# Layer norm's input of units 1 and 2: from TensorE's transposes to VectorE's 32 by 32 turns through DRAM, with a new order table

## The chip, the cores and the metric

The program runs on one core of a Trainium2 chip. The metric is the device time of one execution in microseconds (us). Engines: TensorE (PE), VectorE (DVE), ScalarE (ACT), GpSimd (POOL) and SyncE (SP, which here issues all DMAs).

## The reference

Attention with pooled keys and values (8 batches, 8 heads, 576 positions, 64 wide), then two blocks on the 4608 x 512 rows that it gives. Cut to what matters here:

```python
k_p = k.reshape(B, H, S // 8, 8, D).mean(axis=3)       # v_p likewise
attn = softmax(q @ k_p.T / sqrt(D))
x = (attn @ v_p) as 4608 rows of 512
h = x @ w_in                                           # 512 -> 1024
e = h * softmax(h)
ln = (e - mean(e)) / sqrt(var(e) + 1e-6) * g_ln
x = ln @ w_out                                         # 1024 -> 512
out = ((x @ w1) * (x @ w2)) @ w3 @ w_out2
```

## The kernel before, in words

Every product of float32 numbers is made of three products of rounded halves (high by high, high by low, low by high), so each operand of PE has a high and a low tile (winh, winl, xh, xl, lnh, lnl, gwh, gwl).

The first stage, up to about 590 us, works in 18 **units** of 256 rows, each of two halves (row blocks) of 128 rows. Attention runs two groups ahead in the same stage: per group it turns the queries (`pq`, L598), makes scores (`sc`, L617), their maximum and exponentials (L635, L638), divides (on DVE, L653 and L654, and POOL, L658 and L665), transposes the result on PE (`pt`, L683 and L686), splits it (ACT L690 and L691, DVE L694 and L695), and multiplies by the values (`av`, L722), whose result is split (L216, L217) and copied (L729) as xh and xl. Beside it DVE, ACT and POOL convert weights, those of the last block (w1, w2) in 16 "kept" pieces (L289 to L304), which go to DRAM.

For one half of a unit, `Rows` does this: `chunk` multiplies x by w_in in four steps (L753, tile h, one pair of banks for all halves); `exp` takes the maximum (DVE, L761) and the exponential (ACT, L762); `solu` multiplies (DVE, L768, tile e) and sums squares (ACT, L771). The second product needs e with its 1024 columns on the partitions, and there are two ways:
- **On PE**, `Unit.transpose` (L833): four 128 x 128 transposes into one PSUM bank, an ACT copy that rounds (L836, tile lnh) and a DVE subtraction (L837, tile lnl). A unit takes four such groups.
- **Turned**, for units in TURNED: `turn` lets DVE turn 32 x 32 blocks of e (L777) into a tile that also receives the squares of `solu` and exists once; `send` writes it to DRAM (L784, on SP); three slots later `fetch` reads it back in four DMAs that put the blocks in their places (L791); `part` then rounds it on ACT (L823) and subtracts on DVE (L824).

`Unit.chunk` makes the second product (L847 to L849, 48 matmuls of 256 columns for half of the output columns), `store` copies it out (L859) and sends it (L860).

The program is written by **slots**, 16 to a unit, in the pattern of HEAVY: four slots for the first half's chunks of the unit, four for one half of the second product (x), four for the second half's chunks, four for the other half of the second product (y). For a unit below AT_ONCE both halves of its second product stand in the next unit's slots; for a later one the first half stands in the next unit's last four slots, and the second in the unit after. So with AT_ONCE = 3 the x slots of unit 4 hold no second product.

The order in which each engine gets its instructions is then set by hand: `issue_order` reads ISSUE_ORDER, one list for each engine. An entry "skip:count" moves on by skip in the order of the slots and takes the next count instructions. Each engine, and SP's queue of DMAs, works its list in order, so an instruction that waits holds up all behind it.

Of the kernel before, what the change touches and what calls it, by code (L numbers as in the profile page):

```python
# [128 lines left out]
def attention_moe_kernel(  # L129
# [106 lines left out]

    SLOTS = 16
    LEAD = 2  # L240
    HEAVY = "hhhhxxxxHHHHyyyy"
    AT_ONCE = 3
    TURNED = range(AT_ONCE, NU - 1)
    events = {}
    now = None

    def put(slot, fn, *args, first=5):
        assert now is None or slot > now
# [1299 lines left out]
```

## Time and profile before

| | us |
|---|---|
| median of 3 runs | 1176.77 (1175.39 to 1178.05) |
| the profiled execution, its own time | 1180.64 |
| its span, first to last instruction | 1178.8 |
| PE busy in the span | 1138.8 |
| DVE, ACT, POOL busy | 918.6, 545.3, 526.0 |

Busy time of an engine is time in which it executes; times of a row count from the span's start. In a window the number behind x is that of instructions, and the granted clock is a share of TensorE's full speed. "<-" behind idle time names what ended it.

### The profile page before, as it was taken

What the parts mean: (1) busy time and instruction counts of PE and PEld (TensorE: products, weight loads), DVE (VectorE), ACT (ScalarE), POOL (GpSimd) and SP (SyncE); (2) the same over time, 40 slices, a digit from 0 to 9 for tenths busy, and PEclk for the clock granted to TensorE, in tenths of its full rate; (3) what the DMA queues carried; (4) which work ended last, traced back from release to release, by engine and by line L of the source; (5) the groups of instructions that cost most, each with busy time, mean ns of one, the idle gap of its engine ahead of it and who ended that gap; (6) DMA issues with size and microseconds to landing.
All of it is one profiled execution on the core that took longest, in us unless ns stands there. A gap on an engine that the chain in (4) does not pass through costs nothing. (4 is left out here: it accounts for less than half of the span.)

```text
span 1178.8 us, 20225 instructions
## 1 busy us (share of the span) xinstructions
PE 1138.8 (97%) x7210; PEld 1023.1 (87%) x7210; DVE 918.6 (78%) x1376; ACT 545.3 (46%) x1399; POOL 526.0 (45%) x482
## 2 busy tenths in 40 slices
PE   6898989999999999999989999999999989999998
PEld 4688878999989899999989888888888878999998
DVE  5899879889777775696669769989785677988972
ACT  5665657576656565555522122131130145454542
POOL 2554545555232321100066657676652264555620
PEclk9999999999999999999999999999999999999999
DMA  9675477879474722366254625536441362354501
GB/s 259 155 137 155 126 190 203 229 224 223 133 173 132 170 90 90 133 199 196 79 163 149 200 81 178 195 109 197 136 141 54 116 250 73 108 198 129 174 37 73
DMA packets 167205, 178.56 MB, mean 151 GB/s; under 512 B 82624, under 2 KB 107200, under 8 KB 167104
## 3 DMA queue, kind: packets, MB, share of 16 engines
q1 hardware_dynamic: 167104, 177.26, 51.0%
q8 instruction: 57, 0.93, 0.3%
q14 instruction: 44, 0.36, 0.1%
HBM read 114.30 MB, written 62.91 MB: 150 GB/s over the span
## 5 line engine op out<-in xcount | busy, mean ns | idle before, releaser
L847 PE MATMUL x<-lnh,gwh 128*128 128x256 f32 x576 | 164.3, 285 | 0.5 <-ACT gwh L375 0.5
L849 PE MATMUL x<-lnh,gwl 128*128 128x256 f32 x576 | 161.3, 280 | 0.4 <-DVE gwl L376 0.4
L848 PE MATMUL x<-lnl,gwh 128*128 128x256 f32 x576 | 161.0, 280 | 0.0
L638 ACT ACTIVATE ea<-sc,mx 128x72 f32<-128x72 f32 x320 | 98.7, 325 | 24.9 <-DVE mx L635 20.9
L847 PEld LDWEIGHTS x<-lnh,gwh 128*128 128x128 f32 x576 | 108.5, 188 | 1.7 <-ACT gwh L375 0.7
L848 PEld LDWEIGHTS x<-lnl,gwh 128*128 128x128 f32 x576 | 108.4, 188 | 0.9
L849 PEld LDWEIGHTS x<-lnh,gwl 128*128 128x128 f32 x576 | 108.3, 188 | 0.9 <-DVE gwl L376 0.8
L658 POOL TENSOR_TENSOR pr<-ea,sm 128x512 f32<-128x512 f32 x40 | 41.8, 1044 | 138.3 <-DVE sm L654 78.4
L1156 ACT ACTIVATE p<-p 128x512 f32<-128x512 f32 (+1 forms) x40 | 22.2, 555 | 173.8 <-PE p L1154 146.9
L1168 POOL TENSOR_TENSOR a<-a,b 128x512 f32<-128x512 f32 (+1 forms) x40 | 51.6, 1291 | 101.5 <-issue 61.6
L753 PE MATMUL h<-winh,xh 128*128 128x512 f32 x288 | 95.5, 411 | 0.0
L753 PE MATMUL h<-winl,xh 128*128 128x512 f32 x288 | 90.8, 395 | 0.0
L753 PE MATMUL h<-winh,xl 128*128 128x512 f32 x288 | 90.1, 394 | 0.0
L638 ACT ACTIVATION_READ_ACCUMULATOR ea<-sc,mx 128x1 f32 x320 | 67.4, 211 | 0.0
L762 ACT ACTIVATE e<-h,ST 128x1024 f32<-128x1024 f32 x36 | 40.2, 1118 | 55.9 <-DVE ST L761 55.7
L753 PEld LDWEIGHTS h<-winl,xh 128*128 128x128 f32 x288 | 54.3, 189 | 12.0
L753 PEld LDWEIGHTS h<-winh,xl 128*128 128x128 f32 x288 | 54.1, 189 | 11.8
L1152 PE MATMUL p<-th,w1h 128*128 128x512 f32 (+1 forms) x160 | 59.3, 371 | 2.2 <-DVE a L1162 2.2
L1153 PE MATMUL p<-th,w1h 128*128 128x512 f32 (+1 forms) x160 | 59.1, 369 | 0.0
L1154 PE MATMUL p<-th,w1l 128*128 128x512 f32 (+1 forms) x160 | 59.1, 369 | 0.0
L768 DVE SCALAR_TENSOR_TENSOR e<-h,e 128x1024 f32<-128x1024 f32 x36 | 44.0, 1222 | 16.6 <-ACT e L762 16.4
L1172 POOL TENSOR_TENSOR a<-a,b 128x512 f32<-128x512 f32 (+1 forms) x40 | 55.0, 1376 | 1.2 <-DVE a L1171 1.2
(281 smaller groups left out, 3792.4 us busy)
## 6 DMA issues: line engine op xcount, KB each, us to landing
raw<-pd SPq DMA_DIRECT2D x18, 1024.0 KB
pd<-a SPq DMA_DIRECT2D x64, 256.0 KB
ed<-turn SPq DMA_DIRECT2D x28, 512.0 KB
back<-ed SPq DMA_DIRECT2D x112, 128.0 KB
x2d<-xo SPq DMA_DIRECT2D x35, 256.0 KB
kv<-in_k_dram SPq DMA_DIRECT2D x32, 256.0 KB
kv<-in_v_dram SPq DMA_DIRECT2D x32, 256.0 KB
f<-in_moe_w_dram SPq DMA_DIRECT2D x16, 512.0 KB
```

Of the source, the lines that this page charges most:

```text
L638: nc.scalar.activation(e[0:n, x], half[a][:, h], AF.Exp, bias=mx[0:n, x : x + 1], scale=1.0, accum_out=sm[0:n, x : x + 1],)
L658: nc.gpsimd.tensor_tensor(pr[0:n, 0 : H * KM].rearrange("p (h k) -> p h k", h=H), e[0:n, :, 0:KM], s8.to_broadcast([n, H, KM]), ALU.mult,)
L753: nc.tensor.matmul(self.ph[:, a], s_[:, c], w_[:, c, a * 512 : a * 512 + 512], start=first, stop=last)
L768: nc.vector.scalar_tensor_tensor(e, self.hv, -1.0 / F, e, ALU.mult, ALU.mult, accum_out=st[:, 2:3])
L847: nc.tensor.matmul(o, gw[0][:, f, ws], self.th[:, f], start=(f == 0), stop=False)
L848: nc.tensor.matmul(o, gw[0][:, f, ws], self.tl[:, f], start=False, stop=False)
L849: nc.tensor.matmul(o, gw[1][:, f, ws], self.th[:, f], start=False, stop=(f == FC - 1))
L1152: nc.tensor.matmul(o, wh[:, c, fsl], th[:, c], start=c == 0, stop=False)
L1153: nc.tensor.matmul(o, wh[:, c, fsl], tl[:, c], start=False, stop=False)
L1154: nc.tensor.matmul(o, wl[:, c, fsl], th[:, c], start=False, stop=c == 1)
L1168: nc.gpsimd.tensor_tensor(a[:, 0], a[:, 0], b[:, 0], ALU.mult)
L1172: nc.gpsimd.tensor_tensor(a[:, 1], a[:, 1], b[:, 1], ALU.mult)
```

## The change

AT_ONCE goes from 3 to 1, so TURNED begins with unit 1. Units 1 and 2 lose their eight groups of transposes with eight ACT copies and eight subtractions, and get four turns, four sends, 16 fetches, four ACT copies and four subtractions of twice the width. Their second products move half a unit back, and the x slots that hold none are those of unit 2 now. Only the first and the last unit use PE's transposes. The lists of PE, ACT, DVE, POOL and SP are new from about the place where unit 1 comes in; from about unit 9 on the order is that of before. In PE's list the other instructions of the attention and of h follow each other as before, up to the places of the second products of units 1 to 3. The list of DVE is shown in the first three lines that differ.

```diff
@@
     "PE": (
...
-        "15:7 -22:4 18:8 4:8 -12:2 10 -11:2 -30:2 37:9 -46:2 44:34 5:13 -18:4 14 -15 14:17 1 -2 1:428 1 "
-        "-2 1:9 1 -2 1:3 18:7 -25:18 7:98 1:2 -3 2:2432 5 -6:5 1:3441"
+        "15:7 -22:4 18:8 4:8 -12:2 10 -11:2 -30:2 37:9 -46:2 44:34 5:13 -18:4 14 -15 14:13 1 -2 1:40 "
+        "18:10 -28:18 10:16 12:2 -14 31 -19:2 -15:3 24:2 -26:8 45 -28:2 26:12 -54:12 5:24 13:119 21:5 "
+        "-26:12 38 -39:3 36 2:3 -42:6 5:24 2:2 3:581 5 -6:5 1:370 5 -6:5 1:1681 5 -6:5 1:3441"
...
     "DVE": (
...
-        "18:2 -8:2 -3 2 -43:2 33 -34 10 37:2 -23:4 14 4 -5 4 9 -8 -15:3 4 10 -7:2 1 9 -6 18:2 -19:2 3:2 "
-        "-5 5 -2 1 1:2 -9 5 2 1:2 3 -7 9 -4 -3 3 1:2 -5 4:2 13 -13 16 -19 32 -32:2 61 -57:2 -7 2 3:2 -48 "
-        "42 -43 1 46:3 -13:2 7 4 34 -35 19:2 5 -18:2 39 -51:4 13 -14:3 11 5 -18:2 2 1 11 12 6 -30 -3:2 35 "
...
+        "18:2 -8:2 -3 2 -43:2 33 -34 10 37:2 -23:4 14 4 -5 4 10 -9 -15:3 4 11 -8:2 1 10 -6 18:2 -19:2 3:2 "
+        "-5 5 -2 1 1:2 -9 5 2 1:2 3 -7 10 -5 -3 3 2:3 -36 45 -11 -6 20 17 29 -59:2 -7 6:2 -8 2 8:2 2 -26 "
+        "18 6 1:4 -8 12:2 7 11 -12 -28 -49 59 -60 59:2 -8 7 3 -4 5 2 6:2 -14 2 19 -20 27 -23:2 68 -146 "
...
     SLOTS = 16
     LEAD = 2
     HEAVY = "hhhhxxxxHHHHyyyy"
-    AT_ONCE = 3
+    AT_ONCE = 1
     TURNED = range(AT_ONCE, NU - 1)
```

## Rows read from the trace of the kernel before

**Rows 1.** The page: busy time of TensorE with its share, then its busy tenths in 40 slices.
```profile
PE 1138.8 (97%) x7210; PEld 1023.1 (87%) x7210; DVE 918.6 (78%) x1376; ACT 545.3 (46%) x1399; POOL 526.0 (45%) x482
...
PE   6898989999999999999989999999999989999998
```

**Rows 2.** Windows: stretch, length, busy PE, PEld, DVE, ACT, POOL; clock, DMA share, GB/s.
```profile
88.40:118.00 29.60, 26.56 (x179) 24.07 (x178) 27.66 (x50) 16.86 (x55) 13.98 (x17) 1.00 0.59 156
118.00:147.40 29.40, 27.95 (x187) 25.38 (x187) 23.98 (x50) 18.11 (x61) 17.53 (x24) 1.00 0.45 126
147.40:177.00 29.60, 26.26 (x168) 23.17 (x167) 23.14 (x38) 15.81 (x53) 14.20 (x17) 0.94 0.78 189
177.00:206.00 29.00, 27.77 (x177) 24.63 (x176) 27.14 (x54) 21.95 (x79) 16.93 (x25) 1.00 0.71 204
```

**Rows 3.** Single lines' instructions: count, ns min/median/max, first and last start, forms.
```profile
L833 PE MATMUL lt<-ident,e x64: 270/272/328, 69.5 to 575.2; 128*128 128x128 f32 x64
...
L836 ACT ACTIVATE lnh<-lt x16: 575/600/690, 71.3 to 575.5; 128x512 fp32r<-128x512 f32 x16
...
L837 DVE TENSOR_TENSOR lnl<-lt,lnh x16: 642/683/694, 72.0 to 576.1; 128x512 fp32r<-128x512 f32 x16
...
L823 ACT ACTIVATE lnh<-back x28: 1040/1059/1122, 185.5 to 556.9; 128x1024 fp32r<-128x1024 f32 x28
...
L824 DVE TENSOR_TENSOR lnl<-back,lnh x28: 1182/1222/1992, 186.8 to 558.2; 128x1024 fp32r<-128x1024 f32 x28
...
L777 DVE STREAM_TRANSPOSE turn<-e x28: 1202/1245/1248, 171.0 to 545.7; 128x1024 f32<-128x1024 f32 x28
...
L791 SPq DMA_DIRECT2D back<-ed x112: 303/430/876, 176.3 to 553.6; - x112
L791 SPq EVENT_SEMAPHORE  x19: 17/17/4205, 176.2 to 547.4; - x19
```

**Rows 4.** Timeline of PE, unit 2's transposes: start us, us, engine line op, names, count.
```profile
152.23 0.60 PE L833 MATMUL lt<-ident,e 128*128 128x128 f32 x4
152.58 0.71 PE L753 MATMUL h<-winh,xh 128*128 128x512 f32 x2
153.13 0.63 PE L753 MATMUL h<-winl,xh 128*128 128x512 f32 x2
153.60 0.62 PE L753 MATMUL h<-winh,xl 128*128 128x512 f32 x2
```

**Rows 5.** Timeline of PE, the waits behind them: in brackets idle time before, and releaser.
```profile
157.97 0.66 PE L833 MATMUL lt<-ident,e 128*128 128x128 f32 x4 [1.92 <-DVE lnl L837]
159.26 0.66 PE L683 MATMUL pt<-ident,pr 128*128 128x128 f32 x4 [0.64 <-POOL pr L658]
160.70 0.47 PE L686 MATMUL px<-ident,pr 128*128 128x128 f32 x1 [0.78 <-POOL pr L665]
```

**Rows 6.** Windows: the stretch behind these waits, columns as in rows 2.
```profile
160.83:163.50 2.67, 2.67 (x7) 2.12 (x8) 0.90 (x3) 0.28 (x1) 2.51 (x4) 0.50 0.99 181
```

**Rows 7.** Timeline of PE, first and last of 48 matmuls of unit 1's first half.
```profile
125.81 0.28 PE L847 MATMUL x<-lnh,gwh 128*128 128x256 f32 x1
...
131.85 0.28 PE L849 MATMUL x<-lnh,gwl 128*128 128x256 f32 x1
```

**Rows 8.** Timeline of PE, two waits for copies of the attention's output.
```profile
141.78 0.38 PE L722 MATMUL av<-pth,VBDh 128*128 128x320 f32 x1 [1.00 <-DVE X L729]
...
146.99 0.52 PE L683 MATMUL pt<-ident,pr 128*128 128x128 f32 x3 [0.45 <-DVE X L729]
```

**Rows 9.** Timeline of POOL, the multiplication ahead of the attention's transposes.
```profile
124.92 1.04 POOL L658 TENSOR_TENSOR pr<-ea,sm 128x512 f32<-128x512 f32 x1 [1.81 <-ACT lnh L836]
```

**Rows 10.** Timeline of DVE: the product e, then turn and subtraction of unit 3's second half.
```profile
129.09 1.23 DVE L768 SCALAR_TENSOR_TENSOR e<-h,e 128x1024 f32<-128x1024 f32 x1 [0.21 <-ACT e L762]
...
185.16 1.25 DVE L777 STREAM_TRANSPOSE turn<-e 128x1024 f32<-128x1024 f32 x1 [0.28 <-ACT turn L771]
...
198.22 1.21 DVE L824 TENSOR_TENSOR lnl<-back,lnh 128x1024 fp32r<-128x1024 f32 x1
```

131 rows, old and new, of the table ISSUE_ORDER are left out of this document.

## The prediction

> **What bounds the kernel now.** I began with the page: TensorE (PE) is busy for 1138.8 of 1178.8 us, and its slices show where the rest is: the digits of the first six slices waver between 6 and 9, and from the seventh on they stand at 9 but for three slices at 8 [rows 1]. So a change pays only if PE gets less to do, or if PE waits less in about the first 206 us. The windows show that start by stretch [rows 2]: between 118 and 206 us PE is idle for 1.45, 3.34 and 1.23 us, while VectorE (DVE) has 27.66 of 29.6 us filled just before (88 to 118), then 23.98 of 29.4, 23.14 of 29.6 and 27.14 of 29.0. DVE is thus full where the change begins, and has 88.0 - 74.3 = 13.7 us free in the next three windows. The reader is to see two things: PE sets the end, and in this stretch PE is itself held up by chains that run through DVE.
>
> The profiled execution took 1180.64 us (span 1178.8); the median of the three runs shown is 1176.77, 3.9 lower. I work out differences in the profiled execution and take them from the median. 0.2%, about what a measurement of this kernel can tell from no change, is 2.4 us.
>
> **The change, part by part.** Units 1 and 2 lose 32 transposes on PE, eight groups of four. In the timeline a group starts at 152.23 and the next work at 152.58, 0.35 us later, and the pair of h matmuls behind it takes 0.55 us to the next pair, where a pair usually takes 0.47 [rows 4]; 0.43 us a group, 8 x 0.43 = **3.4 us less PE work**. If a group only fills a wait it is worth nothing, so the bounds are 0 and 3.4; most groups stand between matmuls that run without a gap, so I take 3.4.
>
> Unit 2's last group waited 1.92 us for a subtraction of DVE, since its PSUM banks were not free; the attention transposes behind it then waited 0.64 and 0.78 [rows 5]. Right after these waits the granted clock was 0.50, the lower level (1.2 GHz), for 2.67 us [rows 6], in which the work of 1.34 us was done. With the group gone the 1.92 goes for certain, the rest (0.64 + 0.78 + 1.34) only if nothing else is late there: bounds 1.9 and 4.7, I take 4.7, as the new DVE list has no eviction of unit 2 at that place. Two more short waits, 1.00 and 0.45 us for copies of the attention's output (L729), stand at 141.78 and 146.99 [rows 8]; bounds 0 and 1.45, and I take 1.45, since that copy now has less ahead of it on DVE. Gains together: 3.4 + 4.7 + 1.45 = 9.5 us.
>
> Against this, the matmuls that consume unit 1 move half a unit back. Before, the 48 of its first half filled PE from 125.81 to 131.97 without a gap [rows 7]; while they ran, POOL, ACT and DVE got the attention's next steps ready. In the new PE list the attention's transposes follow straight on h of unit 2, then its scores, its value product, and h's second half. I walked down that list with the durations of before, and find five waits.
> - PE reaches the transposes at about 124.5 (125.81 less three groups). Their input is multiplied on POOL from 124.92, the large part ending at 125.96, and POOL itself had waited 1.81 us behind an eviction of unit 1 on ACT (L836) [rows 9] that is gone. Between 0 and 2.3 us, if the two small parts behind it take an estimated 0.7 (they are two eighths of the large one, which took 1.04, and start anew); I take 0.5, as the cause of POOL's delay is removed.
> - The value product waits for the split of these transposes: 0.6 us, between 0 and 1.2, from the same rows.
> - The second half of h needs the bank that DVE's product e frees; it began at 129.09 and took 1.23 [rows 10], so it is free at 130.3, and PE is there at about 128.5. One turn (1.245 us [rows 3]) is now ahead of e on DVE, but less other work. Between 0 and 3; I take 1.3.
> - The moved matmuls need the turned data of both halves of unit 1. The nearest row for the trip is that of unit 3: from the start of the turn at 185.16 to the end of the subtraction at 198.22 + 1.21, 14.3 us [rows 10]. Unit 1's second turn stands just ahead of e, so at about 127.5, and its data would be there at 141.8. PE goes on with h at 129.8 (128.5 + 1.3) and has 24 matmuls of 0.235 [rows 4] and ten narrower ones of the value product, an estimated 0.15 each (between the 0.125 of the x matmuls [rows 7] and 0.235), before it is there, at about 137: a wait of 4.8. In the trip of that row SP waited 4.2 us for the send to land, the longest of 19 [rows 3], so I take 3.5. The lower bound is 0, the upper 4.8 + 4.2 if SP loses that much once more.
> - Group 4's second transposes then wait 0.8 (0 to 2), as they did before.
>
> Losses: 0.5 + 0.6 + 1.3 + 3.5 + 0.8 = 6.7 us. **Sum: 6.7 - 9.5 = -2.8 us.** The other empty half unit, which stood behind unit 2's matmuls, is now full; as PE hardly waited after 163.5 us, that is worth nothing by itself. Matmuls that only move cost nothing in the sum.
>
> On DVE each unit gets two turns (2 x 1.245) and two long subtractions (2 x 1.222) for four short ones (4 x 0.683): +2.2 us, **+4.4 us for both** [rows 3]. I cost this at nothing beyond the waits above, because 13.7 us are free on DVE from 118 to 206 and the new table puts conversions of the kept weights (w1, w2) back: those of slot 22 stand at places 223, 225 and 244 of DVE's list instead of 208, 210 and 211, and the maximum of h of unit 2 at place 205 instead of 209. Without that room the 4.4 us are on the path (first rival). ACT does two copies of 1.06 us for four evictions of 0.60 a unit, 0.3 less [rows 3], hidden. SP issues 20 more DMAs of about 0.43 us, 8.6 us [rows 3], hidden as long as the loads of keys and values behind them are early; a fetch must wait for its own send to land, and holds up the query and key loads queued behind it on SP. POOL's work is unchanged.
>
> One price is seen only in part. The subtraction that reads PSUM never took over 0.694 us in 16 times; the one that reads two SBUF tiles took 1.222 in the middle and up to 1.992 in 28 [rows 3]. The Trainium skill (SBUF — State Buffer, Who interferes with whom) says why: a VectorE instruction with two SBUF inputs and a GpSimd instruction that reads SBUF block each other for their whole length. The trace agrees, with that 1.992; four subtractions at the worst would add 4 x 0.77 = 3.1 us on DVE, and the sum would come to +0.3 instead of -2.8.
>
> **The rivals.** (1) *Slower: DVE becomes the bound.* Its place is DVE between 118 and 206 us. For it: 27.66 of 29.6 us filled just before. Against: the 13.7 us free and the conversions put back. If the free time can't be used, because it lies in waits of the attention's chains that stay, the 4.4 us shift everything behind and swallow the gain: 1176.8 + 4.4 = 1181.2; half used, 1179.0. It decides from the point where under 4.4 of the 13.7 us can be filled. The Trainium skill (VectorE: DVE Perf Modes, Rules for kernel authors) advises TensorE for a 128 by 128 transpose whose result may go to PSUM, which speaks for this rival; no run here has yet shown it for units 1 and 2. Chance 0.25.
> (2) *Same: the transposes were hidden anyway.* PE follows the attention's chain in this stretch, and whatever is taken out becomes a longer wait for POOL, ACT or the trip. Losses of 9.2 us instead of 6.7, well under the 17.5 of all upper bounds, leave -0.3: 1176.5. For it: the waits of 118 to 177 us are all for other engines. Against: the 1.92 and the half clock were waits for the removed work itself. Chance 0.28.
> (3) *More: the trip is early.* If unit 1's data wait for PE, the 3.5 us fall away: -6.3, so 1170.5. Chance 0.12.
> (4) *The table does it, not the turning.* The gain would come from the conversions put back; the time is that of my forecast, so it has no chance of its own here, but must be told apart.
>
> **How the numbers follow.** Forecast, -2.8 us: 1174.0, chance 0.35. Faster by over 0.2% is the forecast and (3), 0.47; within 0.2%, (2), 0.28; slower, (1), 0.25. The forecast's own range runs from 1171.5 to 1174.4, where no change begins. For 8 in 10 the range takes in (2), most of (3) down to 1170.0, and (1) up to 1179.5; about 0.07 is left out below and 0.12 above.
>
> **What would show it.** Right: no wait for lnl by transposes near 158 us, the clock at its higher level where it was 0.50, a wait of some 3 us ahead of unit 1's first moved matmuls at about 137 to 141, and PE without gaps after about 161. If DVE's busy share from 118 to 206 comes near full and PE waits for mx, sm or the splits there, rival 1 is right. If PE's idle time between 118 and 165 has grown by as much as its work fell, it is rival 2. I am wrong altogether if the difference arises after 300 us, where the program is the same.

## The result, and the profile after

The changed kernel takes 1184.24 us (median of 8 runs, 1182.17 to 1189.79) against 1178.11 us (8 runs, 1175.39 to 1181.28): 1.0056 times as long, 95% interval 1.0042 to 1.0069. It is **slower by 0.56%**, some 6.6 us, where 2.8 us less had been forecast. The profiled execution is the quickest of the eight, 1182.17 us with a span of 1180.4, so its trace shows only part of the loss; the run e1 below gives a second trace.

The busy times of the page and the windows from 118 us on, as in [rows 1, 2], with one more stretch behind them; below them that stretch of the kernel before:

```profile
PE 1139.3 (97%) x7178; PEld 1022.2 (87%) x7178; DVE 927.9 (79%) x1376; ACT 542.6 (46%) x1395; POOL 524.5 (44%) x482
```

```profile
118.00:147.40 29.40, 25.43 (x130) 21.01 (x130) 26.91 (x56) 20.25 (x77) 12.46 (x21) 0.94 0.71 204
147.40:177.00 29.60, 29.11 (x212) 27.27 (x211) 21.77 (x34) 17.43 (x60) 13.56 (x18) 1.00 0.76 182
177.00:206.00 29.00, 29.00 (x201) 27.00 (x201) 24.58 (x49) 19.95 (x64) 13.58 (x20) 1.00 0.70 214
206.00:354.00 148.00, 142.81 (x957) 129.78 (x956) 124.43 (x207) 90.12 (x308) 73.04 (x95) 1.00 0.81 208
```

```profile
206.00:354.00 148.00, 147.47 (x1015) 136.62 (x1014) 120.97 (x207) 94.80 (x322) 65.89 (x89) 1.00 0.76 196
```

Up to 206 us the change did much of what was forecast: TensorE is idle for 3.97, 0.49 and 0.00 us in the three windows from 118 us, 4.46 together where it had been 6.02 [rows 2], and it has 32 transposes less to do. The loss stands in the last window, which the prediction had left alone: PE idles 5.19 us from 206 to 354 us, where it had idled 0.53.

The same is seen where both PE lists have the same work behind them but for the 32 transposes (to within two matmuls). A good mark is the small transposes px (L686, now L688) of a piece of the attention. Their starts in the timeline of PE, in us:

| px of piece | before, at | after | e1 | e5 | e7 |
|---|---|---|---|---|---|
| 3_0 | 114.13 | -0.11 | +0.01 | +0.21 | +0.15 |
| 6_0 | 208.81 | -5.00 | -4.76 | -4.13 | -2.42 |
| 6_1 | 216.80 | -3.99 | -4.03 | -4.61 | -2.49 |
| 7_0 | 236.56 | -2.80 | -2.87 | -2.97 | -2.49 |
| 8_1 | 274.25 | -0.46 | -0.88 | -2.46 | -2.49 |
| 10_0 | 324.69 | +0.14 | -1.05 | +0.07 | -2.49 |
| 10_1 | 332.97 | +1.85 | +2.03 | -0.47 | -3.25 |
| 15_2 | 483.29 | +0.77 | +3.07 | -1.47 | -4.16 |

(e5 and e7 are runs of the next section.) At 209 us the changed kernel is 5 us ahead; at 333 us it is 2 us behind. Part of that lead belongs to the execution of before that it is measured against, which was a long one (1180.64 us, median 1178.11): e7, whose lists are those of before up to 332 us, is 2.42 us ahead of it at 209 us as well, so that against e7 the lead is 2.6 us.

The timeline of PE after the change has these waits of over 0.3 us from 120 to 141 us. Behind them it has one of 0.49 us at 172.63 and one of 0.41 us at 223.44, and three long ones, all for pr of an even group's second piece:

```profile
127.86 0.41 PE L724 MATMUL av<-pth,VBDh 128*128 128x320 f32 x1 [1.19 <-ACT ea L640]
...
137.23 0.39 PE L849 MATMUL x<-lnh,gwh 128*128 128x256 f32 x1 [0.71 <-ACT lnh L825]
...
138.18 0.73 PE L619 MATMUL sc<-bdt,qT 128*128 128x144 f32 x4 [0.46 <-DVE X L731]
139.22 0.39 PE L850 MATMUL x<-lnl,gwh 128*128 128x256 f32 x1 [0.31 <-DVE lnl L826]
...
140.93 0.41 PE L685 MATMUL pt<-ident,pr 128*128 128x128 f32 x2 [1.08 <-DVE X L731]
```

```profile
212.31 0.66 PE L685 MATMUL pt<-ident,pr 128*128 128x128 f32 x4 [1.26 <-POOL pr L660]
...
273.29 0.66 PE L685 MATMUL pt<-ident,pr 128*128 128x128 f32 x4 [1.13 <-POOL pr L660]
...
334.31 0.66 PE L685 MATMUL pt<-ident,pr 128*128 128x128 f32 x4 [2.02 <-POOL pr L660]
```

The timeline of POOL shows what pr waited for at 212 us, first after, then before:

```profile
209.59 1.67 POOL L429 TENSOR_TENSOR vl<-vl 128x256 f32<-128x256 f32 x3 [6.13 <-DMA vl<-in_v_dram]
211.21 1.04 POOL L660 TENSOR_TENSOR pr<-ea,sm 128x512 f32<-128x512 f32 x1
```

```profile
214.24 1.05 POOL L658 TENSOR_TENSOR pr<-ea,sm 128x512 f32<-128x512 f32 x1 [3.11 <-DVE sm L654]
215.25 1.20 POOL L665 TENSOR_TENSOR pr<-ea,sm 128x64 f32<-128x64 f32 x2
216.41 1.92 POOL L427 TENSOR_TENSOR vl<-vl 128x256 f32<-128x256 f32 x3
```

After the change GpSimd first adds up the last rows of V of the **next** batch (vl, L429; the expectations below call it a product), and for that it stands 6.13 us until their load has landed; pr, which PE is waiting for, is behind it in the queue. Before, pr came first and vl second. At all three long waits (1.26, 1.13 and 2.02 us) vl stands ahead of pr. At the third it did so in the table of before too, where PE waited 0.53 us; what has grown there is the wait for the load, which SP issued 1.3 us later (326.10 against 324.83) and which landed 1.9 us later (timeline of POOL after, then before):

```profile
331.59 1.66 POOL L429 TENSOR_TENSOR vl<-vl 128x256 f32<-128x256 f32 x3 [8.97 <-DMA vl<-in_v_dram]
```

```profile
329.73 1.68 POOL L427 TENSOR_TENSOR vl<-vl 128x256 f32<-128x256 f32 x3 [7.09 <-DMA vl<-in_v_dram]
```

So the new order table, not the turning, was now the suspect.

### The profile page after: what moved, and what is told of

It reads as the page before. It is cut to its first block, busy times and chain, and to the rows that moved or that the text cites. A ratio compares the mean times of both kernels' runs of the same rounds, so it can differ in the third digit from the quotient of the medians.

```text
span 1180.4 us, 20181 instructions
## 1 busy us (share of the span) xinstructions
PE 1139.3 (97%) x7178; PEld 1022.2 (87%) x7178; DVE 927.9 (79%) x1376; ACT 542.6 (46%) x1395; POOL 524.5 (44%) x482
## 5 line engine op out<-in xcount | busy, mean ns | idle before, releaser
L1170 POOL TENSOR_TENSOR a<-a,b 128x512 f32<-128x512 f32 (+1 forms) x40 | 50.6, 1266 | 106.7 <-issue 63.9
L755 PEld LDWEIGHTS h<-winh,xh 128*128 128x128 f32 x288 | 50.6, 191 | 6.7 <-DVE e L770 0.2
```

The costliest lines, as they stand in the source:

```text
L755: nc.tensor.matmul(self.ph[:, a], s_[:, c], w_[:, c, a * 512 : a * 512 + 512], start=first, stop=last)
L1170: nc.gpsimd.tensor_tensor(a[:, 0], a[:, 0], b[:, 0], ALU.mult)
```

## The experiments

All edits but those of e10 and e11 are in the order table alone. They are shown decoded: a list's instructions by their names, the slot behind @, "..." for what is left out.

| run | median us (range, runs) | before beside it | ratio (95%) |
|---|---|---|---|
| e1 | 1183.37 (1181.54 to 1187.36, 6) | 1177.21 | 1.0055 (1.0039 to 1.0071) |
| e2 | 1192.52 (1190.58 to 1192.90, 4) | 1177.21 | 1.0125 (1.0112 to 1.0139) |
| e3 | 1193.63 (1189.87 to 1194.59, 4) | 1177.21 | 1.0141 (1.0126 to 1.0156) |
| e4 | 1198.70 (1197.85 to 1200.03, 4) | 1177.21 | 1.0182 (1.0169 to 1.0196) |
| e5 | 1177.92 (1175.98 to 1184.59, 12) | 1177.54 | 1.0005 (0.9991 to 1.0018) |
| e6 | 1184.52 (1180.67 to 1187.56, 6) | 1177.54 | 1.0056 (1.0035 to 1.0078) |
| e7 | 1176.54 (1175.11 to 1179.02, 12) | 1177.54 | 0.9992 (0.9982 to 1.0003) |
| e8 | 1181.10 (1177.35 to 1185.11, 12) | 1177.54 | 1.0027 (1.0014 to 1.0040) |
| e9 | 1176.77 (1173.00 to 1181.21, 12) | 1177.82 | 0.9987 (0.9973 to 1.0001) |
| e10 | 1172.61 (1171.99 to 1173.49, 6) | 1177.82 | 0.9946 (0.9927 to 0.9965) |
| e11 | 1172.36 (1171.41 to 1174.21, 6) | 1177.82 | 0.9947 (0.9928 to 0.9965) |
| e12 | 1173.59 (1171.72 to 1175.87, 12) | 1177.38 | 0.9964 (0.9953 to 0.9975) |

**e1: the changed kernel again.** No edit.

> The changed kernel once more, unaltered, beside the others: both theories expect 1182 to 1188 us, 0.3 to 0.8% over the kernel before, and in its profile the idle time of TensorE from 206 to 354 us at 5.2 us or more (0.5 before the change). Theory P (put back): the turning saves some 5 us from 118 to 206 us, and the conversions of the kept weights that the new table put back into 206 to 354 us lose all of it and more. Theory T (turning): the turning itself, its DMA traffic and its work on VectorE, is what costs, wherever the conversions stand.

It repeats the loss. Its trace has a longer wait for pr, in the timeline of PE, and behind it, in the windows, the lower clock:

```profile
333.70 0.66 PE L685 MATMUL pt<-ident,pr 128*128 128x128 f32 x4 [2.60 <-POOL pr L660]
```

```profile
336.00:339.00 3.00, 3.00 (x15) 2.82 (x14) 1.27 (x2) 0.94 (x1) 1.27 (x2) 0.50 1.07 224
```

So one such place can cost 2.60 us of waiting and then 3 us at a granted clock of 0.50, worth 1.5 us of work. Both traces are of the quickest execution of their kernel; where the slower ones lose more is not shown.

**e2 to e4: conversions moved by the clock.** The first theory was that the conversions of the kept weights cost the time at their new places. They were moved to other times: every step was inserted in its engine's list where the trace had that time.

```diff
 e2, GpSimd's list
 pr3_2<-ea3_2,sm3_2@36
+cvb<-cvb,cvm@24
 KL8<-KL8,KL8@59
+cvb<-cvb,cvm@37
 KL8<-KL8,KL8@59
...
```

> The changed kernel with the conversions of the kept weights at the times they had before the change (118 to 291 us, not 149 to 344). P: TensorE's idle time from 206 to 354 us falls from 5.2 us to under 2; from 118 to 206 us VectorE has the 4.4 us of turning on top of the conversions, so up to 3 us of the gain there may go; 1176 to 1181 us. T: 1183 us or more, with the idle time in 206 to 354 us unchanged.

```diff
 e3, GpSimd's list
 KL8<-KL8,KL8@59
-cvb<-cvb,cvm@24
-cvb<-cvb,cvm@37
-cvm<-f64@48
-cvb<-cvb,cvm@50
 pr4_0<-ea4_0,sm4_0@44
...
```

> The kernel before, not turned, with the conversions at the times of the changed kernel. P: TensorE's idle time from 206 to 354 us rises from 0.5 to 3 to 5 us, and the room on VectorE from 118 to 206 us gives back 0 to 2; 1179 to 1183 us. T: no slower than before, 1176 to 1178 us.

```diff
 e4, GpSimd's list
 kv3_0<-kv3_0,kv3_0@63
-cvb<-cvb,cvm@37
+cvm<-f64@22
+cvb<-cvb,cvm@24
 kv3_1<-kv3_1,kv3_1@67
+cvm<-f64@35
+cvb<-cvb,cvm@37
 pr5_0<-ea5_0,sm5_0@60
...
```

> The changed kernel with the 16 conversions spread from 155 to 472 us, each placed behind an odd group's start, where VectorE and GpSimd have room, and none between the last of a batch's value splits and the next batch's first product. P: TensorE hardly waits from 206 to 354 us (under 1.5 us), the gain of 118 to 206 us stays: 1173 to 1177 us, below both kernels. T: 1183 us or more.

All three lost 14 to 21 us, which neither theory had expected; they decide nothing between the two. What they show is how such a loss comes about. In e2 ScalarE stood first 1.36 us for a conversion's load, later 6.56 us for unit 1's data (timeline of ACT), and PE 4.51 us for ScalarE (timeline of PE):

```profile
136.97 0.69 ACT L294 ACTIVATE cvb<-f 128x512 f32<-128x512 f32 x1 [1.36 <-DMA f<-in_moe_w_dram]
144.22 1.06 ACT L826 ACTIVATE lnh<-back 128x1024 fp32r<-128x1024 f32 x1 [6.56 <-DMA back<-ed]
```

```profile
145.34 0.58 PE L850 MATMUL x<-lnh,gwh 128*128 128x256 f32 x1 [4.51 <-ACT lnh L826]
```

In e4, at 426 us, ScalarE stood 3.50 us for a conversion's load, and the exponentials (ea) behind it came late (timeline of ACT); PE waited twice (timeline of PE):

```profile
426.34 0.66 ACT L293 ACTIVATE cvb<-f 128x512 f32<-128x512 f32 x1 [3.50 <-DMA f<-in_moe_w_dram]
426.91 0.31 ACT L640 ACTIVATE ea<-sc,mx 128x72 f32<-128x72 f32 x1
```

```profile
427.36 0.76 PE L619 MATMUL sc<-bdt,QLT 128*128 128x144 f32 x4 [2.07 <-ACT ea L640]
429.76 1.33 PE L619 MATMUL sc<-bdt,QLT 128*128 128x144 f32 x4 [1.65 <-ACT ea L640]
```

In e3 the windows tell another thing: with the conversions gone from there, the kernel that is *not* turned has no idle PE at all from 118 to 147 us; it loses behind that, where they now stand.

```profile
118.00:147.00 29.00, 29.00 (x203) 26.95 (x201) 20.59 (x46) 17.81 (x68) 10.36 (x18) 1.00 0.27 64
177.00:206.00 29.00, 23.83 (x140) 20.21 (x138) 27.35 (x46) 18.21 (x65) 14.37 (x20) 0.99 0.51 150
```

So places matter more than the amount of work, and the lists have to be compared place by place. Doing that for pr gave the second theory (queue order): in the batches at 212 and 272 us the table of before had pr ahead of vl on GpSimd, pth ahead of vl's rounding (sh) on ScalarE and ptl ahead of sl on VectorE; there ptl also stood ahead of the second pooling of K in the first of them, and sm ahead of the first pooling in the second. The new table has all of it the other way round. In the next two batches both tables have it the wrong way, and there before, too, had waited 0.53 and 0.65 us.

**e5: pr ahead in the changed kernel.** In four batches, on three engines:

```diff
 GpSimd's list
+pr6_1<-ea6_1,sm6_1@81 (three)
 vl4<-vl4,vl4@100 (three)
-pr6_1<-ea6_1,sm6_1@81 (three)
 ScalarE's list
-sh4<-vl4@110
 pth6<-pt6_1@83
 ptx6<-px6_1@83
+sh4<-vl4@110
 VectorE's list
-kp4_0<-kv4_0@92
 sm6_1<-sm6_1@81
 sm6_1<-sm6_1@81
-sl4<-vl4,sh4@110
-kp4_1<-kv4_1@95
+kp4_0<-kv4_0@92
...
 ST<-h5_0@84
+sl4<-vl4,sh4@110
+kp4_1<-kv4_1@95
```

> The changed kernel; for the batches whose next loads land at about 209, 270, 331 and 390 us, GpSimd's product of the last rows of V (which waits for that load) goes behind pr of the second piece instead of ahead of it, and with it the rounding of V's rows on ScalarE and the pooling of K on VectorE. Nothing else moves. Theory Q (queue order): the new table left these three queues in an order in which a load of the next batch stands ahead of pr; TensorE's waits of 1.26, 1.13 and 2.02 us for pr (4.4 us together, 5.9 in the repeat) fall under 1 us together, and the time comes to 1177 to 1180 us. P (conversions put back): the wait at 334 us stays at 2 us or more; 1181 to 1183. T (the turning): 1183 us, no change.

**e6: the reverse, in the kernel before.** In its main moves the mirror image of this diff, at 6_1 and 8_1 only.

> The reverse, in the kernel before: in the two batches at 212 and 272 us, where its table had pr ahead, the product of V's last rows, its rounding and the pooling of K are put ahead of pr, as the new table has them. Q: waits of about 1.3 and 1.1 us for pr appear at those places, 1178.5 to 1181 us. P and T: 1177 us, no change, as the conversions stay and nothing more is turned.

e5 brings back the loss, 1.0055 to 1.0005; e6 makes the same loss, 1.0056, in a kernel in which nothing more is turned. In e5 the timeline of POOL has pr at 209.04, before the load is in, and PE has no wait for pr left behind 206 us:

```profile
209.04 1.04 POOL L660 TENSOR_TENSOR pr<-ea,sm 128x512 f32<-128x512 f32 x1 [4.81 <-DVE sm L656]
...
210.56 2.06 POOL L429 TENSOR_TENSOR vl<-vl 128x256 f32<-128x256 f32 x3
```

In e6 the waits appear where the table had been right (timeline of POOL, then of PE):

```profile
215.55 1.65 POOL L427 TENSOR_TENSOR vl<-vl 128x256 f32<-128x256 f32 x3 [3.46 <-DMA vl<-in_v_dram]
217.16 1.04 POOL L658 TENSOR_TENSOR pr<-ea,sm 128x512 f32<-128x512 f32 x1
```

```profile
218.25 1.12 PE L683 MATMUL pt<-ident,pr 128*128 128x128 f32 x4 [2.67 <-POOL pr L658]
...
279.90 0.66 PE L683 MATMUL pt<-ident,pr 128*128 128x128 f32 x4 [2.07 <-POOL pr L658]
```

2.67 + 2.07 = 4.74 us, more than expected, and the rest of its 7.0 us is mostly the lower clock behind the first (granted 0.81 and 0.63 in the two windows of 3 us from 216). The queue order is thus shown as the cause, from both sides. Both edits move three queues at once, so the share of each is not separated; the waits that come and go are PE's for pr on GpSimd.

**e7: pr ahead also where the kernel before had it wrong.** The diff of e5, at 10_1 and 12_1.

> The kernel before, with pr put ahead in the two batches (at 332 and 391 us) where its own table still had the load's product first. Q: its two waits of 0.53 and 0.65 us go, 1175.5 to 1177 us. P and T say nothing of it: 1177 us.

As expected, PE no longer idles from 206 to 354 us (windows), and the marks gain 0.76 and 0.9 us at 10_1 and 12_1; the time is 0.08% lower, with an interval that still takes in no change.

```profile
206.00:354.00 148.00, 148.00 (x1021) 137.54 (x1020) 121.57 (x207) 95.88 (x332) 65.96 (x90) 1.00 0.76 195
```

**What is left: e8 to e11.** With both tables right, turned and not turned stand at 1177.92 and 1176.54, and e5 still falls from 4.61 us ahead to 0.07 behind. Its waits (PE), and for the second the ScalarE queue:

```profile
223.31 0.76 PE L619 MATMUL sc<-bdt,qT 128*128 128x144 f32 x4 [0.92 <-DVE xl L219]
...
315.93 0.42 PE L724 MATMUL av<-pth,VBDh 128*128 128x320 f32 x1 [1.18 <-ACT ea L640]
```

```profile
309.47 0.68 ACT L293 ACTIVATE cvb<-f 128x512 f32<-128x512 f32 x1 [4.22 <-DMA f<-in_moe_w_dram]
310.05 0.36 ACT L692 ACTIVATE pth<-pt 128x256 fp32r<-128x256 f32 x1
```

At 309 us a conversion's load again: 4.22 us, with pth of the attention behind it. e8 moved the last conversion on:

```diff
 VectorE's list
-cvb<-cvb@222
 turn8_1<-e8_1@142
...
 turn9_0<-e9_0@150
+cvb<-cvb@222
+cvb<-cvb@222
 xl10<-av10_0,xh10@151
+cvb<-f64,cvb@223
```

> As the first of these four, and the last of the 16 conversions, whose VectorE steps stood at 309 to 336 us just ahead of the value splits of K and V, is moved some 25 us on. Q alone: the same time as the first of these four, within 1 us. P beside Q: 1 to 2 us under it, since the splits on VectorE end some 1.3 us earlier at 323 us.

It cost 0.22% more than e5 instead, since the conversion now stood ahead of the split xl, and PE waited 2.70 us for that (timeline of PE):

```profile
347.55 0.76 PE L620 MATMUL sc<-bdt,qT 128*128 128x144 f32 x4 [2.70 <-DVE xl L220]
```

e9 put the last two conversions only into idle stretches of each engine, and one at 218 us behind the product e:

```diff
 VectorE's list
+e5_0<-h5_0,e5_0@85
 cvb<-cvb@102
 cvb<-cvb@102
 cvb<-f64,cvb@103
-e5_0<-h5_0,e5_0@85
...
 mx11_1<-sc11_1_1@157
+cvb<-cvb@209
+cvb<-cvb@209
 turn9_1<-e9_1@158
...
```

> The changed kernel with pr ahead, as in the run that had 1177.92 us, and three conversions moved in their queues: at 217 to 219 us one conversion's steps go behind the product e on VectorE, and the two whose loads landed at 309.5 us, where ScalarE and VectorE stood waiting for them with the attention's steps queued behind, go to 336 to 371 us, into idle stretches of each engine. Theory P2 (conversions put back into places ahead of the attention's steps cost the rest): TensorE's waits of 0.92 us at 223 and 1.18 us at 316 go, with them up to 2.3 us that were lost from 308 to 325; 1174.5 to 1176.5 us, below the kernel before. Rival (the turned units' own work on VectorE is the rest): 1177 to 1179 us, the waits come back elsewhere.

1176.77, with an interval (0.9973 to 1.0001) that reaches just to no change. No new wait came behind 330 us, but the one at 223 us stayed, and another conversion's chain now made PE wait, 1.38 us at 296.84 for the exponentials, so the expectation held only in part.

e10 (from e5) and e11 (from e7) leave the conversions' engine work out; their loads and stores stay, at the places that each table gives them:

```diff
+    class Skipped(Kept):
+        def bits(self):
+            pass
...
+        def store(self):
+            nc.sync.dma_start(piece(self.to, self.i), at(win[0], self.i % 8).bitcast(F32))
...
     bg = bg[:EARLY_PIECES]
+    for pc in bg:
+        pc.__class__ = Skipped
```

> The changed kernel with pr ahead, and with the 16 conversions' steps on ScalarE, VectorE and GpSimd left out (their loads stay, and their stores write words of another weight): what the turning alone is worth shows against the same in the kernel before. P2: no waits from 206 to 354 us, and the lead of 4 to 5 us that the turning had at 209 us is kept: 3 to 5 us under the kernel before without conversions, 1170 to 1173 us. Rival (hidden anyway): within 1 us of it.

> The kernel before with pr ahead in its two batches, and the same steps left out. P2: its waits of 1.9, 0.6 and 0.8 us at 157 to 160 us and the lower clock behind them partly stay, as they are waits for the transposed units' evictions: 1174 to 1176 us. Rival (the gain up to 206 us came from the conversions put back, not from the turning): 1170 to 1173 us, as fast as the turned one without conversions.

1172.61 and 1172.36: with the conversions' work out of the way **the turning by itself is worth nothing in these order tables**. The rivals in both expectations were right: the gain up to 206 us came from the conversions put back, and e12 below, which is not turned, has it too (px of 6_0 5.40 us earlier than in the kernel before). The windows of e10, then e11, show how the 3.4 us of transposes were paid back:

```profile
118.00:147.00 29.00, 24.37 (x123) 20.11 (x122) 25.43 (x50) 20.22 (x77) 12.42 (x21) 0.94 0.66 189
147.00:177.00 30.00, 29.51 (x212) 27.53 (x211) 18.75 (x31) 16.06 (x57) 8.61 (x13) 1.00 0.81 194
177.00:206.00 29.00, 29.00 (x202) 27.01 (x201) 20.17 (x40) 17.70 (x57) 7.96 (x15) 1.00 0.71 209
```

```profile
118.00:147.00 29.00, 29.00 (x201) 26.88 (x200) 19.42 (x44) 17.75 (x67) 10.46 (x18) 1.00 0.52 144
147.00:177.00 30.00, 28.21 (x194) 25.42 (x192) 19.09 (x30) 15.68 (x59) 9.55 (x15) 1.00 0.89 228
177.00:206.00 29.00, 27.68 (x182) 25.05 (x181) 23.82 (x48) 21.21 (x75) 8.52 (x15) 1.00 0.68 184
```

From 118 to 206 us PE idles 4.63 + 0.49 + 0.00 = 5.12 us turned and 0.00 + 1.79 + 1.32 = 3.11 us not turned, 2.0 more; and turned it runs from 118 to 147 us at a mean granted clock of 0.94, 0.06 x 29 = 1.7 us lost, which the other does not lose. 2.0 + 1.7 = 3.7 for the 3.4 saved.

Part of that is again queue order. In all the turned kernels ScalarE's list has the copy of unit 1's second half (lnh) ahead of a split of the attention (xh). In the timeline of ACT after the change it stands 3.64 us for the turned data, and xh comes behind it, though the value product that xh splits was over at about 135.3 us:

```profile
136.12 1.06 ACT L825 ACTIVATE lnh<-back 128x1024 fp32r<-128x1024 f32 x1 [3.64 <-DMA back<-ed]
137.09 0.36 ACT L218 ACTIVATE xh<-av 128x256 fp32r<-128x256 f32 x1
```

VectorE's half of the split waits 1.33 us for xh, with the copy X behind it in the list, and PE's 0.46 us for X at 138.18 follows from that; its 1.08 us at 140.93 probably does too. In e10 the copy stands 4.56 us, with the same two waits. Whether the turning would gain something with xh ahead was not tried.

**e12: a faster kernel.** If room on the other engines from 118 us on is what pays, the kernel before can have it without turning. Each of the first ten conversions takes the place of the one six later; the last six go into idle stretches from 345 to 485 us:

```diff
 GpSimd's list
 cvb<-cvb,cvm@22
-cvm<-f64@22
-cvm<-f64@35
 kv2_0<-kv2_0,kv2_0@31
...
 VectorE's list
 mx13_1<-sc13_1_1@189
+cvb<-cvb@182
+cvb<-cvb@182
 turn11_1<-e11_1@190
...
```

> The kernel before (nothing more turned) with pr ahead in its two batches, and the conversions of the kept weights moved back by six: each of the first ten stands where the one six later stood (180 to 291 us), the last six go to idle stretches at 345 to 485 us. What is left of the theories: the room on VectorE, ScalarE and GpSimd from 118 to 180 us, not the turning, is what pays, as the two kernels without conversions were equal. Then TensorE's idle time from 118 to 206 us falls from 4.9 us to near the 3.1 us of the kernel without conversions, with no new waits behind it: 1173 to 1175.5 us, below both kernels. If the conversions cost the same wherever they stand: 1176.5 us.

```profile
118.00:147.00 29.00, 29.00 (x201) 26.92 (x200) 19.50 (x45) 17.78 (x67) 10.53 (x18) 1.00 0.27 63
147.00:177.00 30.00, 28.07 (x191) 25.26 (x191) 21.05 (x33) 15.98 (x60) 12.55 (x18) 1.00 0.80 194
177.00:206.00 29.00, 27.99 (x183) 24.97 (x182) 27.48 (x54) 23.27 (x80) 13.30 (x20) 1.00 0.67 175
206.00:354.00 148.00, 148.00 (x1010) 136.96 (x1009) 121.41 (x210) 95.58 (x337) 66.73 (x92) 1.00 0.77 202
```

1173.59 us, 0.36% under the kernel before (0.9953 to 0.9975) and 0.9% under the changed one (1.0056 / 0.9964, each measured beside the kernel before). PE idles 2.94 us from 118 to 206 us and not at all up to 354.

## Why the prediction was wrong

**The step that failed** is the one that costed the new table behind 206 us at nothing. The sum has no term there: "as PE hardly waited after 163.5 us, that is worth nothing by itself" and "after 300 us, where the program is the same" took it for granted that what had not waited would not wait. But the lists of GpSimd and VectorE differ up to about 336 us. At 212 and 272 us PE had not waited because the old table kept pr ahead of the next batch's load, and the old POOL rows could not show that as a price, only its absence. "POOL's work is unchanged" was true of the amount and not of the order. The lists were walked on PE and VectorE up to unit 2 and not on GpSimd and ScalarE behind it. Measured, putting pr ahead is worth 0.50% of the time (e5 against e1), 5.9 us of the 9.4 between the forecast (-2.8) and the result (+6.6); in two of its four batches the table of before had the wrong order too, which cost that kernel 0.53 and 0.65 us of waits.

The other 3.5 us are a gain that was counted for the turning and is not there. With pr ahead the changed kernel is level with the kernel before (1.0005) and not 2.8 us faster, and without the conversions' work turned and not turned are level too (e10, e11). The lead at 209 us, 2.6 us against e7, is close to the 2.8 forecast by luck: it came from the conversions put back, not from the terms of the sum.

Point by point, up to 206 us:
- *Transposes, 3.4 us.* They were gone, but e10 and e11 show that nothing of it is left over: the mechanism of the second rival ("hidden anyway"), though not its forecast of the time.
- *Waits of [rows 5] and the lower clock, 4.7 us.* The waits went, 3.34 us. The lower clock came elsewhere: after the change it is 0.58 and 0.86 in the windows from 141 us, behind the waits shown above, which is 1.7 us of work and was in no term. The 1.34 us of [rows 6] are not the kernel's for certain: with the same order there e6 loses much the same again (0.63 and 0.80 in its two windows of 3 us from 159), and e7 loses nothing (last section).

```profile
141.00:144.00 3.00, 3.00 (x15) 2.72 (x16) 2.85 (x7) 2.44 (x11) 1.51 (x3) 0.58 0.70 199
144.00:147.00 3.00, 3.00 (x13) 2.43 (x12) 3.00 (x4) 1.67 (x10) 0.00 (x0) 0.86 1.01 316
```

- *Waits for X, 1.45 us* [rows 8]. Not gained: 0.46 and 1.08 us are still waited for X.
- *Losses, 6.7 us.* Too high by themselves, and nearly right with the 1.7 us of lower clock. In place of 0.5 + 0.6 + 1.3 + 3.5 + 0.8 the windows show 3.97 us from 118 to 147: no wait for pr at 124 us, 0.23 for the split, none for the bank of h, 0.71 + 0.31 for the turned data, 1.54 for X. One of 1.19 had been overlooked: the second half of the value product waits until ScalarE has read the scores (ea), probably for their bank. The turn began at 126.41 and not at 127.5, and the trip took 12.8 us (the subtraction ended at 137.96 + 1.22) and not 14.3; PE came to it at 136.5, as forecast. The 4.2 us of SP's waiting were misread: in the trip of that row SP issued an output and five query loads between the send (186.89) and the fetch (191.08), with 0.1 us free ahead of the fetch; its waits of over 4 us for a send stand at 429 and 547 us. Part of the trip's price came by another way, as the waits for X behind lnh on ScalarE.
- *VectorE's 4.4 us at nothing.* Right in that stretch: from 141 to 206 us PE waits only once, 0.49 us for ea, and VectorE's busy time there is 26.91 + 21.77 + 24.58 = 73.3 us, no more than the 74.3 of before. So rival 1, whose 1181.2 us came nearest, named the wrong place. But the room came from conversions that were only put off, and with pr ahead some of that came due: e5 loses 4.7 us of its lead from 217 to 325 us, at conversions, and e9 and e12 show that places without such a loss exist. Rival 4 ("the table does it") was right about the place of the gain, and did not see that the same table would lose it.

The advice weighed in rival 1, the Trainium skill's (VectorE: DVE Perf Modes, Rules for kernel authors) for TensorE's transposes, is neither borne out nor contradicted here: e10 and e11 differ by 0.25 us, within their scatter.

What stays open: whether the turned kernel would reach e12's time with its conversions placed as there. It was not tried; e10 and e11 speak for the same time, not a better one, as long as lnh stands ahead of xh.

## What to carry to other kernels

When a change brings a new order, compare the orders of **all** queues over the whole stretch in which they differ, not only where work was added: look above all for an instruction that waits for a load standing ahead of one that the bounding engine waits for. A stretch without idle time says that its order is good, not that order is free there. And before crediting a gain to work that is removed, take out the work that was moved at the same time from both versions, as e10 and e11 did.

## What was not expected of the hardware

The subtraction with two SBUF inputs stretched further than the 1.992 us of [rows 3], in the changed kernel up to 2.873 (columns as there):

```profile
L826 DVE TENSOR_TENSOR lnl<-back,lnh x32: 1181/1224/2873, 130.0 to 558.8; 128x1024 fp32r<-128x1024 f32 x32
```

The Trainium skill (SBUF — State Buffer, Who interferes with whom) gives mutual blocking with GpSimd as the reason for such stretching; how much of the 2.873 is that no run here isolates.

The lower clock does not follow each such wait. In e7 PE waited 1.66, 0.64 and 0.78 us at 157 to 160 us, much as in [rows 5], and the granted clock stayed at 1.00 there; with the 1.7 us that the windows of before lose at 159 to 165 us, this one episode makes most of e7's lead of 2.42 us at 6_0.
